# A linear-attention and top-1 MoE block on one core: low parts moved to VectorE, statistics to ScalarE, and a unit's last transposes moved behind two products

## The chip, the core and the metric

The kernel runs on one core of a Trainium2 chip. The core has five engines that run beside each other, each through its own list of instructions in order: TensorE (PE, matrix products; PEld is its loading of the stationary operand), VectorE (DVE), ScalarE (ACT), GpSimd (POOL) and SyncE (SP, which only issues transfers here). They wait for each other through semaphores. Data lies in HBM, in the on-chip memory SBUF (128 partitions), and in PSUM, where TensorE leaves its results in banks. The metric is the device time of one launch in microseconds; less is better.

## The reference

The input x has 2048 tokens of 512 numbers. The block is attention and then a mixture of experts, each added to its input:

```python
h  = x + A(layernorm(x))          # 32 heads of 16
h2 = h + B(layernorm(h))          # 8 experts, one per token

# A: q, k, v = x @ wqkv;  pq = q @ w_phi[head], pk = k @ w_phi[head]
#    phi = concat(softmax(p), softmax(-p))              over the 16 of a head
#    num = phi_q @ (phi_k^T v);  den = phi_q . sum(phi_k) + 1e-6
#    out = (num / den) @ wo
# B: expert = argmax(x @ w_gate);  out = silu(x @ w1[e]) @ w2[e]   (512 -> 1792 -> 512)
#    times a softmax over the one kept logit
```

## The kernel before

**Products in three parts.** Operands of the large products are split into a high part in the fp32r format (an ACT copy, `hi_of`) and the low rest (a subtraction, `lo_of`), and each product is three matmuls: high by high, high by low and low by high (`mm3`, the lines 75 to 77). So every activation and every weight needs one pass on ACT and one subtraction, mostly on DVE.

**Attention.** The 2048 tokens are sixteen chunks of 128. For each chunk the first loop (`s_ln`, `s_tr`, `s_k`, `s_v`, `s_q`, `feat1`, `feat2`, `s_kv`, `s_qt`) normalises x, transposes it, forms k, v, q, and the softmax features; `s_kv` adds phi_k^T v and the sums of phi_k into `kvps` in PSUM. The value product also carries eight more columns, the gate's weights applied to the normalised x (`xwg`), and `s_v` adds a correction with x's mean and the column sums `csg` of the gate on POOL.

**Second half and routing.** A second loop runs over c from 0 to 23 with stages in a pipeline: `s_num(c)` forms num and den and divides, `s_ot(c-1)` transposes and splits the result (PE `pto`, ACT `xh`, DVE `xl`), and `s_wo(c-2)` multiplies by wo (`po`; its PSUM tile has one buffer, so the next one waits until DVE has read it), adds x to give h (`hb`), forms gate logits `lg`, takes mean and variance of h by bn_stats and bn_aggr (`ln_rstd`), and corrects the logits by the mean. Each pair of chunks then has `s_top` (argmax, a one-hot `oh`, running counts `cum`, the gate on POOL, and a transfer of h to `hbuf` in HBM), `s_rank` (each token's rank in its expert: the small products `pl`; then one-hot rows `am` and `bm`) and `s_inv` (a product `acc` that builds the inverse list of tokens by expert). After half the tokens, `s_star` picks the commonest expert so far; the transfers of its weights `raw` start, and at c = 12 to 15 `split_chunk` splits four chunks of them (2048 columns each, in four pieces of 512), with ten of the sixteen low parts on POOL and six on DVE. `s_first` gathers that expert's first 128 tokens, and `prework(0)` normalises them on DVE (`xn`) and transposes them (`mtr`).

**Units.** A unit is 128 tokens of one expert; 19 run here. A unit has the first product in four blocks of columns (`gemm1`, tile `mh`), silu on ACT (`hs`), transposes of each block (`tr`: PE `mtr`, ACT `hThi`, DVE `hTlo`), and the second product (`g2`, tile `my`) of fourteen steps of three matmuls; DVE scales and adds h (`yo`), and POOL scatters the rows to the output. A unit also transposes the next unit's input (`prework(u + 1)`), and, where the next unit has a new expert, splits that expert's weights (`split`, in a branch that is taken by a flag). The PSUM tiles `mh` and `mtr` share four banks in turn (`bank`).

**What sets the order.** The program is written in the order of the loops; a scheduler then places the instructions on each engine's list within what their dependencies allow, so the lists do not follow the source line by line. Each list is fixed when the program is built.

Of the kernel before, what the change touches and what calls it, by code (L numbers as in the profile page):

```python
# [9 lines left out]
F32 = mybir.dt.float32  # L10
# [31 lines left out]
def kernel(  # L42
# [19 lines left out]
    def bc(ap, n):  # L62
        return ap.unsqueeze(len(ap.shape)).to_broadcast(list(ap.shape) + [n])
# [26 lines left out]
    G.iota(iotaS, pattern=[[P, NT]], base=0, channel_multiplier=0, allow_small_or_imprecise_dtypes=True)  # L90
    tok1 = consts.tile([P, NT], F32, name="tok1")
    G.iota(tok1, pattern=[[P, NT]], base=1, channel_multiplier=1, allow_small_or_imprecise_dtypes=True)
# [74 lines left out]

    LO = (V,) * NW

    def split_chunk(c, lo=None, n=2):  # L170
        for i in range(n):
            w = slice(i * (CW // n), (i + 1) * (CW // n))
            hi_of(whi[c][:, w], raw[c][:, w])
            eng = lo or LO[c]
            eng = eng[i] if isinstance(eng, tuple) else eng
            eng.tensor_tensor(wlo[c][:, w], raw[c][:, w], whi[c][:, w].bitcast(F32), op=OP.subtract)  # L176

# [14 lines left out]
    with ExitStack() as actx:  # L192
# [10 lines left out]
        wolo = keep.tile([P, KD, 2, HC], F32R, name="wolo")  # L203
        csg = keep.tile([P, 2, E // 2], F32, name="csg")
        xwg = keep.tile([P, NT, 2, E // 2], F32, name="xwg")
        kvbd = keep.tile([P, NG, 68], F32, name="kvbd")
        V.memset(kvbd, 0.0)
# [53 lines left out]
        def s_num(c):  # L261
            load_x(c)
            o = row("o", 2, "pc").rearrange("p (h f) -> p h f", f=DH)
            for i in range(2):
                pn = bank("pn")
                for g in range(4):
                    T.matmul(pn[:, g * 68:(g + 1) * 68], phT[c][:, 4 * i + g, :], kvbd[:, 4 * i + g, :],  # L267
                             start=True, stop=True)
                nv = pn[:, 0:272].rearrange("p (h f) -> p h f", f=DH + 1)
                den = work.tile([P, 16, 1], F32, name="den")  # L270
                V.tensor_scalar(den, nv[:, :, DH:DH + 1], 1e-6, None, op0=OP.add)
# [10 lines left out]
        if True:  # L282
# [116 lines left out]
            for k in range(KD):  # L399
                T.matmul(pc[:, 0:E], onesf, wgs[:, k, :], start=(k == 0), stop=(k == KD - 1))  # L400
            V.tensor_copy(csg.rearrange("p i e -> p (i e)"), pc[:, 0:E])

# [6 lines left out]
            for c in range(NT - 1):  # L409
# [7 lines left out]
                if c == 3:  # L417
                    pg = bank("pog")
                    for dt in range(KD):
                        for t in range(4):  # L420
                            T.matmul(pg[:, dt * E:(dt + 1) * E], woT_raw[t // 2][:, t % 2, dt * P:(dt + 1) * P],
                                     wgs[:, t, :], start=(t == 0), stop=(t == 3))
                    split_w(wo_raw, pg[:, 0:KD * E].rearrange("p (t i e) -> p t i e", t=KD, i=2), wohi, wolo)
# [33 lines left out]
        def s_wo(c):  # L457
# [11 lines left out]
            V.tensor_tensor(lg, po[:, :, D // 2:HC], xwg[:, c], op=OP.add)  # L469
            ln_rstd(h[:, 0:D], h[:, D:D + 2], h[:, D + 1:D + 2])  # L470
            V.scalar_tensor_tensor(lg, csg, h[:, D:D + 1], lg, op0=OP.mult, op1=OP.subtract)

        def s_top(b):
            hb, lg = bt[b]["hb"], bt[b]["lg"]
            mn = work.tile([P, NB, 1], F32, name="tmn")
            V.tensor_reduce(mn, lg, AX.X, OP.min)
            eq = work.tile([P, NB, E], F32, name="eq")
            V.tensor_tensor(eq, lg, mn.to_broadcast([P, NB, E]), op=OP.is_equal)
            V.tensor_tensor(eq, eq, mid(desc8, NB), op=OP.mult)
# [9 lines left out]
            nr = work.tile([P, NB, 1], F32, name="nr")  # L489
            V.tensor_reduce(gt[:, 0], mn, AX.X, OP.min)  # L490
            G.tensor_tensor(gt[:, 0], gt[:, 0], mn, op=OP.subtract)
            G.tensor_tensor(gt[:, 0], gt[:, 0], hb[:, :, D + 1:D + 2], op=OP.mult)
# [6 lines left out]
        def s_rank(b):  # L499
# [16 lines left out]
            bm = work.tile([P, NB, E, NT], F16, name="bm")  # L516
            for j in range(NB):
                c = b * NB + j
                V.tensor_scalar(am[:, j, :], iota128, sl[:, j:j + 1], None, op0=OP.is_equal)
                jm = work.tile([P, NT], F16, name="jm")  # L520
                V.tensor_scalar(jm, iotaS, bs[:, j:j + 1], tok1[:, c:c + 1], op0=OP.is_equal, op1=OP.mult)
                V.tensor_tensor(bm[:, j], bc(oh[:, j, :], NT), mid(jm, E), op=OP.mult)
            bt[b]["am"], bt[b]["bm"] = am, bm
# [33 lines left out]
        for c in range(NT + 8):  # L557
# [60 lines left out]
    def load_fl(a, b):  # L618
        _, v = nc.values_load_multi_w_load_instructions(isnew[0:1, a:b],
                                                        engines=[ENG.Activation, ENG.DVE, ENG.Pool])  # L620
        fls.update(zip(range(a, b), v))
# [97 lines left out]
    def unit(u):  # L719
# [43 lines left out]
        if u == 0:  # L763
            tr(3)
            split_chunk(4, V)
            with after(first_[0]):
                split_chunk(5, V)
                g2(py, 0, 8)
                xi = prework(1)
            with after(xi):  # L770
                split_chunk(6, V)
                index(3, 4, raw[1])
# [6 lines left out]
        else:  # L779
            if u + 1 < NU:  # L780
# [73 lines left out]
```

## Time and profile before

| | us |
|---|---|
| median of 3 runs | 735.6 (734.75 to 735.78) |
| the profiled execution | 732.92 |
| its span, first to last instruction | 731.2 |
| PE busy in the span | 702.0 |
| DVE busy | 468.8 |
| ACT busy | 303.2 |
| POOL busy | 180.8 |

"Busy" is the time in which an engine had an instruction in work. Matmuls are pipelined and overlap, so a busy PE can still be waiting in part; the granted clock tells how fast PE was allowed to run. In rows of groups, the numbers behind the bar are the time all instructions of a group were busy, the mean of one in ns, and the idle time of the engine just before them with what ended it. In rows of the timeline they are the start and the duration in us.

### The profile page before, as it was taken

How to read it: one execution, taken by the hardware profiler on the slowest of the kernel's cores; microseconds unless marked ns; L12 is line 12 of the kernel's file. 1: busy time of each engine (PE TensorE's matmuls, PEld its weight loads, DVE VectorE, ACT ScalarE, POOL GpSimd, SP SyncE). 2: the span in 40 equal slices, each digit the busy share in tenths (PEclk: the TensorE clock that was granted, in tenths of full speed). 3: DMA queues.
4: the chain of work that ended last, by engine and by line, in shares of the span. 5: the costliest groups of instructions: out<-in, count | busy, mean ns of one | idle time of the engine just before them, and what ended most of it. 6: DMA issues, size and time to landing. Idle time of an engine off the chain costs nothing.

```text
span 731.2 us, 12523 instructions
## 1 busy us (share of the span) xinstructions
PE 702.0 (96%) x4130; PEld 612.2 (84%) x4130; DVE 468.8 (64%) x969; ACT 303.2 (41%) x458; POOL 180.8 (25%) x281
## 2 busy tenths in 40 slices
PE   6999999999999998779999999999999999999996
PEld 6899999999989997658888888888888878888885
DVE  4996987878787889794512999972185472922211
ACT  4534444434322015152112888862274463822211
POOL 3364645434313328521110011110011111011110
PEclk9999999999999999899999999999999999999999
DMA  9111101100002249417400799981066381001000
GB/s 332 57 30 44 30 15 30 30 15 1 1 16 73 74 156 341 153 34 294 193 29 2 258 369 376 344 345 53 30 210 241 121 328 31 11 29 30 30 30 6
DMA packets 21912, 87.61 MB, mean 120 GB/s; under 512 B 3070, under 2 KB 3582, under 8 KB 14656
## 3 DMA queue, kind: packets, MB, share of 16 engines
q1 hardware_dynamic: 18624, 76.86, 28.8%
q0 software_dynamic: 3200, 9.75, 4.0%
q8 instruction: 34, 0.56, 0.3%
q14 instruction: 54, 0.44, 0.2%
HBM read 78.18 MB, written 9.21 MB: 120 GB/s over the span
## 4 chain that ended last, share of the span: by engine, by line
issue 46%; PE 35%; DMA 10%; DVE 6%; POOL 1%; ACT 1%; POOLq 1%; SPq 0%; DVEq 0%
DMA out_dram<-yo,sidx 8%; PE kvps L372 4%; PE pn L267 3%; PE pq L75 2%; PE pq L77 2%; PE pq L76 2%; PE ptq L381 2%; PE pv L77 2%; PE pv L76 2%; PE pv L75 2%; PE pk L75 2%; PE pk L77 2%; PE pk L76 2%; PE po L75 2%; PE po L76 2%
## 5 line engine op out<-in xcount | busy, mean ns | idle before, releaser
L69 ACT ACTIVATE whi<-raw 128x1024 fp32r<-128x1024 f32 (+1 forms) x120 | 118.7, 1003 | 67.9 <-PE mh L77 37.4
L176 DVE TENSOR_TENSOR wlo<-raw,whi 128x1024 fp32r<-128x1024 f32 (+1 forms) x110 | 130.6, 1200 | 18.6 <-ACT whi L69 12.5
L75 PE MATMUL mh<-whi,xhi 128*128 128x512 f32 (+1 forms) x304 | 114.9, 378 | 0.0
L77 PE MATMUL mh<-whi,xlo 128*128 128x512 f32 (+1 forms) x304 | 111.5, 367 | 0.0
L76 PE MATMUL mh<-wlo,xhi 128*128 128x512 f32 (+1 forms) x304 | 111.4, 366 | 0.0
L798 POOL DMA_INDIRECT out_dram<-yo,sidx x19 | 21.5, 1131 | 352.5 <-DVEq L635 202.0
L76 PE MATMUL my<-wlo,hThi 128*128 128x512 f32 x266 | 104.7, 393 | 3.5 <-DVE wlo L176 3.3
L75 PE MATMUL my<-whi,hThi 128*128 128x512 f32 x266 | 106.0, 399 | 0.3 <-ACT hThi L69 0.3
L77 PE MATMUL my<-whi,hTlo 128*128 128x512 f32 x266 | 104.6, 393 | 0.3 <-DVE hTlo L72 0.3
L72 DVE TENSOR_TENSOR hTlo<-mtr,hThi 128x512 fp32r<-128x512 f32 x76 | 47.0, 621 | 86.2 <-ACTq L635 53.3
L163 ACT ACTIVATE hs<-mh 128x512 f32<-128x512 f32 x76 | 41.0, 540 | 145.3 <-PE mh L77 145.3
L355 POOL TENSOR_TENSOR ph<-t,sm 128x1024 f32<-128x1024 f32 x32 | 62.1, 1939 | 66.9 <-DVE sm L353 37.8
L77 PEld LDWEIGHTS mh<-whi,xlo 128*128 128x128 f32 x304 | 57.2, 188 | 10.2
L76 PEld LDWEIGHTS mh<-wlo,xhi 128*128 128x128 f32 x304 | 57.3, 189 | 9.3
L75 PEld LDWEIGHTS mh<-whi,xhi 128*128 128x128 f32 x304 | 57.2, 188 | 9.3
L797 DVE SCALAR_TENSOR_TENSOR yo<-my,xg 128x512 f32<-128x512 f32 x19 | 14.2, 748 | 78.4 <-PE my L77 78.4
L76 PEld LDWEIGHTS my<-wlo,hThi 128*128 128x128 f32 x266 | 50.3, 189 | 14.2 <-DVE wlo L176 4.3
L77 PEld LDWEIGHTS my<-whi,hTlo 128*128 128x128 f32 x266 | 50.3, 189 | 11.2 <-DVE hTlo L72 0.5
L75 PEld LDWEIGHTS my<-whi,hThi 128*128 128x128 f32 x266 | 50.4, 189 | 10.5 <-ACT hThi L69 0.5
L352 DVE TENSOR_REDUCE sm<-t 128x64 f32<-128x1024 f32 x32 | 38.8, 1214 | 12.0 <-ACT t L347 11.9
L727 PE MATMUL mtr<-ident,hs 128*128 128x128 f32 x266 | 41.7, 274 | 2.7 <-DVE hTlo L72 2.6
L347 ACT ACTIVATE t<-t 128x1024 f32<-128x1024 f32 x32 | 33.9, 1061 | 20.9 <-DVE t L346 19.8
(206 smaller groups left out, 1407.3 us busy)
## 6 DMA issues: line engine op xcount, KB each, us to landing
raw<-in_w_dram SPq DMA_DIRECT2D x56, 1024.0 KB, 5.2
xt<-in_x_dram SPq DMA_DIRECT2D x32, 256.0 KB, 2.7
hbuf<-hb SPq DMA_DIRECT2D x8, 516.0 KB, 3.8
phT<-in_wqkT_dram SPq DMA_DIRECT2D x4, 512.0 KB, 5.1
phT<-in_wv_dram SPq DMA_DIRECT2D x2, 512.0 KB, 6.4
phT<-in_wo_dram SPq DMA_DIRECT2D x2, 512.0 KB, 8.2
phT<-in_woT_dram SPq DMA_DIRECT2D x2, 512.0 KB, 5.6
xg<-hbuf,gidx POOLq DMA_INDIRECT x21, 3.7
```

Of the source, the lines that this page charges most:

```text
L69: A.activation(dst, src, AF.Copy)
L72: V.tensor_tensor(dst, src, hi.bitcast(F32), op=OP.subtract)
L75: T.matmul(ps, ahi, bhi, start=first, stop=False)
L76: T.matmul(ps, ahi, blo, start=False, stop=False)
L77: T.matmul(ps, alo, bhi, start=False, stop=last)
L163: A.activation(hs[c % 2][:, 0:fw], p[:, 0:fw], AF.Silu)
L176: eng.tensor_tensor(wlo[c][:, w], raw[c][:, w], whi[c][:, w].bitcast(F32), op=OP.subtract)
L347: A.activation(t, t, AF.Exp)
L352: V.tensor_reduce(sm, t, AX.X, OP.add)
L355: G.tensor_tensor(ph.rearrange("p (a f) -> p a f", f=DH), t, bc(sm, DH), op=OP.mult)
L372: T.matmul(kvps[g // 4][:, g % 4, :], ph[:, g * P:(g + 1) * P], vt[:, 4 * g:4 * g + 4, :].rearrange("p h f -> p (h f)"), start=(c == 0 and ...
L727: T.transpose(pt[:, j * P:(j + 1) * P], hs[c % 2][:, j * P:(j + 1) * P], ident)
```

## The change

It has seven edits. (1) `split_chunk` uses `lo_of` for all low parts, so POOL does none; POOL is taken out of the flags that the branches read. (2) In `s_wo`, h's mean and variance come from two ACT passes with a summed output (a copy, and a square of h minus the mean), with small POOL steps between and after them that form the negative mean, the mean, the variance plus epsilon and its power. (3) The gate's weights have their column mean subtracted before they go through wo (`wgc`), so that the corrections by the mean of x and of h, and the negation, are gone; the argmax looks for the largest logit. (4) The epsilon of the denominator is added to `kvbd` once instead of to each `den`. (5) The one-hot rows of two chunks are made by four instructions on both at once. (6) `tok1` is float16. (7) In a unit, `tr(3)` stands after `g2(py, 0, 2)`.

```diff
-    LO = (V,) * NW
-    def split_chunk(c, lo=None, n=2):
+    def split_chunk(c, n=2):
         for i in range(n):
             w = slice(i * (CW // n), (i + 1) * (CW // n))
             hi_of(whi[c][:, w], raw[c][:, w])
-            eng = lo or LO[c]
-            eng = eng[i] if isinstance(eng, tuple) else eng
-            eng.tensor_tensor(wlo[c][:, w], raw[c][:, w], whi[c][:, w].bitcast(F32), op=OP.subtract)
+            lo_of(wlo[c][:, w], raw[c][:, w], whi[c][:, w])
...
-                split_chunk(c - NT + 4, ((G, G, V, V), (G, G, G, V), (G, G, G, V), (G, G, V, V))[c - NT + 4], 4)
+                split_chunk(c - NT + 4, 4)
...
-                V.tensor_scalar(den, nv[:, :, DH:DH + 1], 1e-6, None, op0=OP.add)
-                V.reciprocal(den, den)
+                V.reciprocal(den, nv[:, :, DH:DH + 1])
...
-                mc = work.tile([P, 2, E // 2], F32, name="mc")
-                G.tensor_scalar(mc, csg, st[c]["mv"][:, 0:1], None, op0=OP.mult)
-                G.tensor_tensor(xwg[:, c], xwg[:, c], mc, op=OP.add)
...
+            wgc = wp.tile([P, KD, E], F32, name="wgc")
+            csg = wp.tile([P, E], F32, name="csg")
+            V.tensor_scalar(csg, pc[:, 0:E], 1.0 / D, None, op0=OP.mult)
+            V.tensor_tensor(wgc, wgs, mid(csg, KD), op=OP.subtract)
...
-                    V.tensor_copy(kvbd[32 * h:32 * h + 32, 4 * i:4 * i + 4, 17 * h:17 * h + 17],
-                                  kvps[i][32 * h:32 * h + 32, :, 17 * h:17 * h + 17])
+                    V.tensor_tensor(kvbd[32 * h:32 * h + 32, 4 * i:4 * i + 4, 17 * h:17 * h + 17],
+                                    kvps[i][32 * h:32 * h + 32, :, 17 * h:17 * h + 17],
+                                    epsz[32 * h:32 * h + 32], op=OP.add)
...
-            ln_rstd(h[:, 0:D], h[:, D:D + 2], h[:, D + 1:D + 2])
-            V.scalar_tensor_tensor(lg, csg, h[:, D:D + 1], lg, op0=OP.mult, op1=OP.subtract)
+            junk = row("junk", 3, "xn")
+            sm = work.tile([P, 2], F32, name="hsum")
+            A.activation(junk, h[:, 0:D], AF.Copy, accum_out=sm[:, 0:1])
+            nm = work.tile([P, 1], F32, name="hnm")
+            G.tensor_scalar(nm, sm[:, 0:1], -1.0 / D, None, op0=OP.mult)
+            G.tensor_scalar(h[:, D:D + 1], sm[:, 0:1], 1.0 / D, None, op0=OP.mult)
+            A.activation(junk, h[:, 0:D], AF.Square, bias=nm, accum_out=sm[:, 1:2])
+            ve = work.tile([P, 1], F32, name="ve")
+            G.tensor_scalar(ve, sm[:, 1:2], 1.0 / D, EPS, op0=OP.mult, op1=OP.add)
+            G.tensor_tensor(h[:, D + 1:D + 2], ve, nhalf, op=OP.pow)
...
-            for j in range(NB):
-                c = b * NB + j
-                V.tensor_scalar(am[:, j, :], iota128, sl[:, j:j + 1], None, op0=OP.is_equal)
-                jm = work.tile([P, NT], F16, name="jm")
-                V.tensor_scalar(jm, iotaS, bs[:, j:j + 1], tok1[:, c:c + 1], op0=OP.is_equal, op1=OP.mult)
-                V.tensor_tensor(bm[:, j], bc(oh[:, j, :], NT), mid(jm, E), op=OP.mult)
+            jm = work.tile([P, NB, NT], F16, name="jm")
+            V.tensor_tensor(jm, mid(iotaS, NB), bc(bs, NT), op=OP.is_equal)
+            V.tensor_tensor(jm, jm, bc(tok1[:, b * NB:(b + 1) * NB], NT), op=OP.mult)
+            V.tensor_tensor(bm, bc(oh, NT), jm.unsqueeze(2).to_broadcast([P, NB, E, NT]), op=OP.mult)
+            V.tensor_tensor(am, mid(iota128, NB), bc(sl, P), op=OP.is_equal)
...
                 prework(u + 1)
+            g2(py, 0, 2)
             tr(3)
-            g2(py, 0, 2)
```

More of the change, by code (lines that the diff above doesn't have):

```diff
@@ L90 @@
     G.iota(iotaS, pattern=[[P, NT]], base=0, channel_multiplier=0, allow_small_or_imprecise_dtypes=True)
-    tok1 = consts.tile([P, NT], F32, name="tok1")
+    tok1 = consts.tile([P, NT], F16, name="tok1")
     G.iota(tok1, pattern=[[P, NT]], base=1, channel_multiplier=1, allow_small_or_imprecise_dtypes=True)
@@ L203 @@
         wolo = keep.tile([P, KD, 2, HC], F32R, name="wolo")
-        csg = keep.tile([P, 2, E // 2], F32, name="csg")
         xwg = keep.tile([P, NT, 2, E // 2], F32, name="xwg")
+        epsz = keep.tile([P, 4, DH + 1], F32, name="epsz")
+        V.memset(epsz, 0.0)
+        V.memset(epsz[:, :, DH:DH + 1], 0.5e-6)
         kvbd = keep.tile([P, NG, 68], F32, name="kvbd")
@@ L421 @@
                             T.matmul(pg[:, dt * E:(dt + 1) * E], woT_raw[t // 2][:, t % 2, dt * P:(dt + 1) * P],
-                                     wgs[:, t, :], start=(t == 0), stop=(t == 3))
+                                     wgc[:, t, :], start=(t == 0), stop=(t == 3))
                     split_w(wo_raw, pg[:, 0:KD * E].rearrange("p (t i e) -> p t i e", t=KD, i=2), wohi, wolo)
@@ L469, in s_wo @@
             V.tensor_tensor(lg, po[:, :, D // 2:HC], xwg[:, c], op=OP.add)
-            ln_rstd(h[:, 0:D], h[:, D:D + 2], h[:, D + 1:D + 2])
-            V.scalar_tensor_tensor(lg, csg, h[:, D:D + 1], lg, op0=OP.mult, op1=OP.subtract)
+            junk = row("junk", 3, "xn")
[8 more added lines that the diff above has]
+            G.tensor_tensor(h[:, D + 1:D + 2], ve, nhalf, op=OP.pow)
         def s_top(b):
             hb, lg = bt[b]["hb"], bt[b]["lg"]
-            mn = work.tile([P, NB, 1], F32, name="tmn")
-            V.tensor_reduce(mn, lg, AX.X, OP.min)
+            mx = work.tile([P, NB, 1], F32, name="tmx")
+            V.tensor_reduce(mx, lg, AX.X, OP.max)
             eq = work.tile([P, NB, E], F32, name="eq")
-            V.tensor_tensor(eq, lg, mn.to_broadcast([P, NB, E]), op=OP.is_equal)
+            V.tensor_tensor(eq, lg, mx.to_broadcast([P, NB, E]), op=OP.is_equal)
             V.tensor_tensor(eq, eq, mid(desc8, NB), op=OP.mult)
@@ L489, in s_top @@
             nr = work.tile([P, NB, 1], F32, name="nr")
-            V.tensor_reduce(gt[:, 0], mn, AX.X, OP.min)
-            G.tensor_tensor(gt[:, 0], gt[:, 0], mn, op=OP.subtract)
+            V.tensor_reduce(gt[:, 0], mx, AX.X, OP.max)
+            G.tensor_tensor(gt[:, 0], mx, gt[:, 0], op=OP.subtract)
             G.tensor_tensor(gt[:, 0], gt[:, 0], hb[:, :, D + 1:D + 2], op=OP.mult)
@@ L619, in load_fl @@
         _, v = nc.values_load_multi_w_load_instructions(isnew[0:1, a:b],
-                                                        engines=[ENG.Activation, ENG.DVE, ENG.Pool])
+                                                        engines=[ENG.Activation, ENG.DVE])
         fls.update(zip(range(a, b), v))
@@ L764, in unit @@
             tr(3)
-            split_chunk(4, V)
+            split_chunk(4)
             with after(first_[0]):
-                split_chunk(5, V)
+                split_chunk(5)
                 g2(py, 0, 8)
@@ L770, in unit @@
             with after(xi):
-                split_chunk(6, V)
+                split_chunk(6)
                 index(3, 4, raw[1])
```

1 line of the change is left out of this document (removed).

## The prediction

> **What bounds the kernel now.** I read the page's busy shares, then the sums by stretch of time, the waits of TensorE (PE), and last the timeline where PE is not full.
>
> ```profile
> PE 702.0 (96%) x4130; PEld 612.2 (84%) x4130; DVE 468.8 (64%) x969; ACT 303.2 (41%) x458; POOL 180.8 (25%) x281
> ```
> ```profile
> 26.00:205.00 179.00, 179.00 (x1186) 163.34 (x1184) 144.51 (x232) 74.42 (x118) 82.32 (x115) 0.99 0.07 22
> ...
> 225.00:266.00 41.00, 40.98 (x366) 40.46 (x364) 33.50 (x156) 5.81 (x10) 15.26 (x42) 1.00 0.29 90
> ...
> 280.00:302.20 22.20, 16.56 (x101) 15.35 (x102) 21.43 (x70) 6.26 (x12) 20.30 (x32) 0.77 0.69 245
> 302.20:317.70 15.50, 15.50 (x102) 12.92 (x100) 10.91 (x51) 4.30 (x6) 4.78 (x12) 1.00 0.29 115
> ...
> 336.20:731.20 395.00, 385.51 (x1944) 322.35 (x1942) 198.55 (x265) 180.84 (x260) 39.09 (x37) 1.00 0.41 152
> ```
>
> The columns after the length are PE, weight loads, VectorE (DVE), ScalarE (ACT) and GpSimd (POOL), then granted clock, DMA share and GB/s. PE is full in attention (26 to 205 us), in the output projections (225 to 266) and from 302 to 318. Between 280 and 302, where the first expert's weights are split while the last tokens are routed, DVE is full (21.43 of 22.20), POOL nearly so, PE has 16.56 and a granted clock of 0.77. An edit pays there, or where PE itself waits:
>
> ```profile
> PE mtr L727 <- DVE hTlo L72: 2.6, 7, 0.4
> PE pl L504 <- DVE oh L483: 2.5, 1, 2.5
> PE po L75 <- DVE lg L469: 2.3, 2, 1.9
> ```
>
> The last two lie inside 280 to 302. The first is seven times 0.4 us in the expert units.
>
> **The change, part by part. 1: all low parts on DVE.** Ten of sixteen subtractions leave POOL. First, what they cost DVE today:
>
> ```profile
> 283.67 1.31 DVE L519 TENSOR_SCALAR am<-iota,sl 128x128 f16<-128x128 f32 x1
> ```
> ```profile
> 283.56 3.80 POOL L176 TENSOR_TENSOR wlo<-raw,whi 128x512 fp32r<-128x512 f32 x3
> ```
> ```profile
> L519 DVE TENSOR_SCALAR am<-iota,sl x16: 273/279/1307, 236.9 to 315.8; 128x128 f16<-128x128 f32 x16
> ```
> ```profile
> L471 DVE SCALAR_TENSOR_TENSOR lg<-csg,hb,lg x16: 216/226/1243, 218.1 to 311.2; 128x8 f32<-128x8 f32 x16
> ```
> ```profile
> L479 DVE TENSOR_TENSOR eq<-eq,desc x8: 110/170/1089, 226.7 to 312.9; 128x16 f32<-128x16 f32 x8
> ```
> ```profile
> L222 DVE BATCH_NORM_STATS2 bs<-hb 128x6 f32<-128x512 f32 x3 | 2.1, 695 | 0.0
> ...
> L471 DVE SCALAR_TENSOR_TENSOR lg<-csg,hb,lg 128x8 f32<-128x8 f32 x3 | 1.7, 564 | 0.0
> L519 DVE TENSOR_SCALAR am<-iota,sl 128x128 f16<-128x128 f32 x2 | 1.6, 794 | 0.0
> L521 DVE TENSOR_SCALAR jm<-iotaS,rb,tok 128x16 f16<-128x16 f32 x2 | 1.6, 779 | 0.0
> L522 DVE TENSOR_TENSOR bm<-oh,jm 128x128 f16<-128x128 bf16 x2 | 1.4, 688 | 0.0
> ...
> L479 DVE TENSOR_TENSOR eq<-eq,desc 128x16 f32<-128x16 f32 x1 | 1.1, 1089 | 0.0
> L483 DVE TENSOR_TENSOR oh<-eq,km 128x16 bf16<-128x16 f32 x1 | 0.9, 942 | 0.0
> L271 DVE TENSOR_SCALAR den<-pn 128x16 f32<-128x16 f32 x4 | 0.7, 162 | 0.0
> ```
>
> The last fence groups DVE from 277.5 to 299. An `am` that normally takes 0.28 us takes 1.31 beside a POOL subtraction. With 0.28 as the quiet time of am, jm and bm the surplus is 2 x (0.794 + 0.779 + 0.688) - 6 x 0.28 = 2.84; for lg 3 x (0.564 - 0.226) = 1.01; for eq and oh 1.089 + 0.942 - 2 x 0.17 = 1.69. Together 5.5 us of DVE time that POOL causes.
>
> The Trainium skill (SBUF — State Buffer, section "Who interferes with whom") says that a DVE instruction with two SBUF inputs, or in a two-port mode, and a GpSimd instruction that reads SBUF exclude each other for a whole instruction. On the wide subtractions the trace agrees (1.31 against 0.28).
>
> Now the sum for this stretch, along DVE's order:
>
> ```profile
> 280.13 0.68 DVE L466 TENSOR_TENSOR hb<-po,xt 128x512 f32<-128x512 f32 x1
> ...
> 296.97 0.16 DVE L469 TENSOR_TENSOR lg<-po,xwg 128x8 f32<-128x8 f32 x1
> ...
> 298.38 0.66 DVE L176 TENSOR_TENSOR wlo<-raw,whi 128x512 fp32r<-128x512 f32 x1
> ...
> 299.18 0.54 DVE L144 TENSOR_SCALAR xn<-xg 128x512 f32<-128x512 f32 x1
> ```
> ```profile
> 297.27 0.56 PE L75 MATMUL po<-wohi,xh 128*128 128x260 f32 x1 [1.94 <-DVE lg L469]
> 302.16 0.61 PE L147 MATMUL mtr<-ident,xn 128*128 128x128 f32 x4
> ```
>
> From hb (280.13) to the last lg before the transposes (297.13) are 17.0 us. Off: 5.5 of surplus, and two rounds of statistics and mean correction with the four `den` additions, 2 x 0.695 + 2 x 0.226 + 0.7 = 2.5, of which about 2.2 is start to start. On: in the built order eight low parts stand ahead of that lg instead of two, 6 x 0.66 = 4.0. So lg comes at 17.0 - 5.5 - 2.2 + 4.0 = 13.3 us, 3.7 earlier. xn: 19.05 before; 5.5 and 3.2 (three rounds) off, 8 x 0.66 = 5.3 on, 15.65, so 3.4 earlier, at about 296. The path then runs lg, projection `po`, `mtr`: 302.16 - 297.27 = 4.9 us at the reduced clock. With that clock kept, mtr starts at 298.4, a gain of 3.7. At the full rate `po` takes 24 x 0.12 = 2.9 (two neighbouring products below start 0.12 apart), mtr starts when xn is done at 296.3, and the gain is 5.9.
>
> ```profile
> 291.82 0.28 PE L77 MATMUL po<-wohi,xl 128*128 128x260 f32 x1
> 291.94 0.28 PE L75 MATMUL po<-wohi,xh 128*128 128x260 f32 x1
> ```
>
> I take 4.8, the middle of the two: PE idles less in this stretch but does not stop idling. DVE stays its bound, so nothing hides an instruction there. The ends are 5.9 and, if ACT cannot deliver the high parts in time, 0.
>
> **2: statistics of h on ACT.** Sixteen bn_stats and bn_aggr leave DVE (counted above where DVE is the bound, worth 0 where PE is full). ACT gets 32 passes over 128x512 with a sum; POOL's two small steps per chunk become four.
>
> ```profile
> L69 ACT ACTIVATE xh<-pto 128x512 fp32r<-128x512 f32 x8 | 4.8, 598 | 35.1 <-PE pto L237 25.9 <-DVE den L271 4.6 <-DVE eq L479 4.6
> ```
> ```profile
> L232 ACT ACTIVATE xn<-xt,nbias,rstd 128x512 f32<-128x512 f32 x16 | 13.1, 819 | 17.5 <-POOL nbias L231 17.5
> ...
> L225 POOL TENSOR_SCALAR ve<-hb 128x1 f32<-128x1 f32 x16 | 4.4, 272 | 31.5 <-DVE tmn L476 14.2 <-DVE den L271 6.7 <-DVE rk L509 3.7
> ```
>
> Price of a pass: low 0.60 (the copy xh), high 0.82 (xn, which also scales and shifts) plus a read of the sum, say 0.9; I take 0.75, nearer the plain copy. ACT then has, per chunk in the projection stage, 0.73 (5.81 over 8 xh) plus 1.5 of 5.1 us (41.0 / 8): it is covered by PE's full queue, cost 0. New is a wait inside ACT's order: the second pass waits for POOL's mean, and behind it stand the next chunk's xh, phT and, from 280 on, whi. Who waits for those is PE's `po`, through xl, and DVE's wlo. The mean takes 0.27 on POOL plus queueing; POOL is busy 1.9 us a chunk (15.26 / 8), so the whole is at worst 0.73 + 1.8 + 0.27 + 1.9 = 4.7 us, under 5.1. Between 280 and 302 ACT has 6.26 of 22.2 busy; 8 more passes make 12 or 13. Cost 0, high end in the rivals. The last q features (ph of chunk 15) now stand on POOL behind the statistics of chunk 0, about 1 us later, while PE reaches them a projection later too: 0.
>
> **3: paired one-hots, centred gate weights, epsilon in kvbd.** Six one-hot instructions per pair of chunks become four wider ones; the two sides are within 0.3 us per pair, two pairs in the stretch: 0, ends -0.6 and +0.6. Two small DVE steps at the start replace 32 POOL steps, whose wait on ACT held up only POOL while PE was full (179.00 of 179.00): 0. Eight adds replace eight copies before kvbd: 0. SP's list moves one load of x by one place: 0.
>
> **4: a unit's last transposes behind two products.**
>
> ```profile
> 446.32:468.23 21.91, 21.53 (x110) 17.90 (x109) 20.63 (x23) 18.74 (x24) 2.72 (x2) 1.00 0.92 358
> 509.24:530.59 21.35, 21.35 (x109) 17.94 (x108) 4.30 (x7) 4.51 (x9) 2.00 (x2) 1.00 0.08 25
> ```
> ```profile
> 433.24 0.68 DVE L72 TENSOR_TENSOR hTlo<-mtr,hThi 128x512 fp32r<-128x512 f32 x1
> ...
> 530.59 0.75 DVE L797 SCALAR_TENSOR_TENSOR yo<-my,xg 128x512 f32<-128x512 f32 x1 [7.47 <-PE my L77]
> ```
> ```profile
> 434.07 0.41 PE L727 MATMUL mtr<-ident,hs 128*128 128x128 f32 x2 [0.37 <-DVE hTlo L72]
> ```
>
> The windows run from one yo to the next: a unit that splits the next expert's weights takes 21.91, one that does not 21.35. The 0.56 is the seven-fold wait: the transposes need a PSUM bank that hTlo of the second block frees at 433.92. Six products of 0.23 put ahead of them take 1.4 us and need only the first block of hT; the bank is then free 1.0 us early. Seven units x 0.56 = 3.9. In units without splits the same instructions run, 0. On ACT the last hThi now stands behind the first whi pair (2.1 us) and DVE's hTlo behind that; they are needed by product 12 of 14, 7 us later: hidden. DVE is 20.63 busy of 21.91, so in the run of four such units it may lag 0.2 us more per unit than PE; the 1.0 covers it. Bounds 0 and 3.9; taken 3.8.
>
> **Sum.** 4.8 + 3.8 = 8.6. The profiled execution took 732.9 (span 731.2): 724.3. The runs' median is 735.6, 2.7 above it; from there **727.0 us**.
>
> **The rivals.** (a) The wait in the units is replaced: DVE lags and PE stops at the next bank. For it: DVE's 20.63 of 21.91; against it: three of the seven split units stand alone and can catch up afterwards. 735.6 - 4.8 = 730.8. (b) ACT becomes the bound of the split stretch: whi stands behind statistics that wait for hb and POOL, so DVE gains nothing there. For it: ACT is in order and leads every wlo; against: 13 of 22 us. 735.6 - 3.8 = 731.8. (c) Slower: in the projection stage xh of the next chunk is held back behind the second pass until PE waits for `po`. It decides from 8.6 / 14 = 0.6 us per chunk over 5.1, so when ACT's turn reaches 5.7; at 6.0 it is 14 x 0.9 = 12.6, giving 739.6. For it: POOL's 1.9 us per chunk come in blocks; against: the 4.7 above. (d) Neither works: 735.6. (e) PE's clock is not lowered again: gain 5.9 there, 725.9. (f) POOL's two added steps per chunk hold DVE up as the wide ones did: four chunks in the stretch x 2 x 0.27 = 2.2, giving 729.2. Against it, beside a small POOL step DVE is not stretched:
>
> ```profile
> 300.77 0.82 POOL L493 TENSOR_TENSOR gt<-euler,gt 128x2 f32<-128x2 f32 x1
> ```
> ```profile
> 300.75 0.28 DVE L522 TENSOR_TENSOR bm<-oh,jm 128x128 f16<-128x128 bf16 x1
> ```
>
> [...]
>
> **How the numbers follow.** Forecast with (e): 0.55; (a) 0.09; (b) 0.12; (f) 0.05; (d) 0.05; (c) 0.14. Alone, the forecast spans 725 to 729. The range 723.5 to 732.5 takes in (a), (b) and (f), 0.81, with 1.5 us below (e) for one-hots that come out cheaper and a lowered clock elsewhere. About 0.2% (1.5 us) is what a measurement of this kernel can tell from no change. Faster 0.81, same 0.05, slower 0.14.
>
> **What would show it.** Between the split's first hb and mtr: no wlo on POOL, am near its 0.28 median in every row or once per pair at 128x256 without stretching, mtr near 297. In the units: no row of mtr waiting for hTlo, split units near 21.4. Wrong, if PE's waits list xh or xl in the projection stage (c), if DVE's waits list whi from 280 on (b), or if a new wait on DVE as long as 0.4 appears in split units (a).

## The result, and the profile after

The changed kernel takes 723.0 us (722.57 to 723.8) against 735.2 beside it (734.17 to 735.78): a ratio of 0.9837 (0.982 to 0.9854), a gain of 12.2 us. Forecast were 8.6 of gain and 727.0 us, range 723.5 to 732.5: the direction and the places are right, the size is too small, and the time lies just below the range. The profiled execution takes 722.8 us (span 721.0).

The busy line of the page, and then the sums by stretch (length, PE, weight loads, DVE, ACT, POOL, clock, DMA share, GB/s):

```profile
PE 697.6 (97%) x4130; PEld 606.6 (84%) x4130; DVE 450.6 (63%) x886; ACT 324.2 (45%) x522; POOL 171.7 (24%) x271
```
```profile
226.50:267.50 41.00, 41.00 (x369) 40.63 (x368) 27.39 (x122) 16.27 (x41) 19.16 (x59) 1.00 0.31 99
278.70:295.13 16.43, 13.58 (x105) 13.05 (x104) 15.12 (x51) 10.44 (x24) 8.64 (x19) 0.91 0.73 273
295.13:311.20 16.07, 15.82 (x103) 13.14 (x103) 10.24 (x53) 7.49 (x15) 7.26 (x20) 0.98 0.32 110
329.62:714.43 384.81, 384.77 (x1944) 321.11 (x1942) 197.18 (x265) 180.07 (x260) 38.14 (x36) 1.00 0.42 157
```

The four rows are the projection stage, the split stretch (from the hb behind which the weights are split to the first mtr), the stretch after it, and the units. The projection stage is as full as before. From the split's hb to the first unit's transposes 22.0 us have become 16.4, DVE still at 92% there. From the first yo to the last, 388.2 have become 384.8, with PE full. PE's waits, the chain that the forecast followed (DVE's and PE's rows), and one split unit from yo to yo:

```profile
PE my L76 <- DVE wlo L72: 3.3, 1, 3.3
PE po L75 <- DVE lg L467: 2.6, 2, 2.1
```
```profile
278.70 0.68 DVE L464 TENSOR_TENSOR hb<-po,xt 128x512 f32<-128x512 f32 x1
...
290.56 0.16 DVE L467 TENSOR_TENSOR lg<-po,xwg 128x8 f32<-128x8 f32 x1
290.63 2.49 DVE L72 TENSOR_TENSOR wlo<-raw,whi 128x512 fp32r<-128x512 f32 x4
...
293.12 0.54 DVE L144 TENSOR_SCALAR xn<-xg 128x512 f32<-128x512 f32 x1
```
```profile
290.86 0.36 PE L75 MATMUL po<-wohi,xh 128*128 128x260 f32 x1 [2.06 <-DVE lg L467]
...
295.13 0.74 PE L147 MATMUL mtr<-ident,xn 128*128 128x128 f32 x3
```
```profile
L527 DVE TENSOR_TENSOR am<-iota,sl x8: 412/418/425, 238.6 to 307.1; 128x256 f16<-128x256 f32 x8
```
```profile
418.09:439.47 21.38, 21.38 (x110) 17.88 (x109) 20.47 (x23) 18.46 (x24) 2.72 (x2) 1.00 0.94 364
```

The wait of mtr for hTlo is gone, the split unit takes 21.38 in place of 21.91, am is never stretched. By stage, with the first row of pn at 205.29 before and 206.83 after: start 1.5 us longer; pn to mtr 96.9 to 88.3; mtr to first yo 34.0 to 34.5; units 388.2 to 384.8. That makes 10.0 of the 10.1 us between the two profiled executions; before's profiled execution lay 2.3 below its median here, which is the rest.

### The profile page after: what moved, and what is told of

Its sections match the earlier page's. It is cut to its first block, busy times and chain, and to the rows that moved or that the text cites. A ratio compares the mean times of both kernels' runs of the same rounds, so it can differ in the third digit from the quotient of the medians.

```text
span 721.0 us, 12308 instructions
## 1 busy us (share of the span) xinstructions
PE 697.6 (97%) x4130; PEld 606.6 (84%) x4130; DVE 450.6 (63%) x886; ACT 324.2 (45%) x522; POOL 171.7 (24%) x271
## 5 line engine op out<-in xcount | busy, mean ns | idle before, releaser
L72 DVE TENSOR_TENSOR wlo<-raw,whi 128x1024 fp32r<-128x1024 f32 (+1 forms) x120 | 135.9, 1151 | 15.8 <-ACT whi L69 8.1
L69 ACT ACTIVATE whi<-raw 128x1024 fp32r<-128x1024 f32 (+1 forms) x120 | 118.1, 1001 | 60.4 <-PE mh L77 43.6
L75 PE MATMUL mh<-whi,xhi 128*128 128x512 f32 (+1 forms) x304 | 114.6, 377 | 0.2 <-ACT xhi L69 0.2
L75 PE MATMUL my<-whi,hThi 128*128 128x512 f32 x266 | 107.7, 405 | 0.2 <-ACT hThi L69 0.2
L69 ACT ACTIVATE hThi<-mtr 128x512 fp32r<-128x512 f32 x76 | 41.1, 542 | 11.7 <-PE mtr L732 11.6
```

The lines of the kernel that those rows point to most:

```text
L69: A.activation(dst, src, AF.Copy)
L72: V.tensor_tensor(dst, src, hi.bitcast(F32), op=OP.subtract)
L75: T.matmul(ps, ahi, bhi, start=first, stop=False)
```

## The experiments

Two numbers are read from each run: its ratio to the kernel before on the same chip, and in its profile the stretch from the first pn (a numerator product of the second half) to the first yo (the first unit's output), 130.9 us before and 122.8 after. Some theories are put for pn to mtr (the first transposes of a unit's input), 96.9 and 88.3. One execution of that stretch is uncertain by some 1.5 us, as the second profile of the changed kernel shows below.

**One edit alone or taken back.** Theories first: the lock by POOL's wide subtractions (T1), or the earlier request for the first expert's weights (T2), which the changed profile shows (267.2 in place of 270.2).

Units only:
```diff
+            g2(py, 0, 2)
             tr(3)
-            g2(py, 0, 2)
```


> The kernel before with one edit: in each unit from the second on, the transposes of the last block stand behind the first two products of the second stage. Theory A (the forecast's term for the units is right, and the rest of the gain is made ahead of them): seven split units x 0.56 us = 3.9, so about 731.3 against 735.2, split units near 21.4 and no transpose waiting for hTlo. Theory B (the 3.4 us that the two profiles show between first and last yo is only part of it, the reordering being worth the 3.6 us by which the forecast fell short as well): 7 us or more, under 728.5. Rival (a) of the forecast: a wait on DVE takes its place, about 735.


Measured: 0.9947 (0.9926 to 0.9969), 3.9 us; pn to first yo 131.1, units 384.7. Theory A: the units' term is right and ends there.

Low parts only:
```diff
...
-                split_chunk(c - NT + 4, ((G, G, V, V), (G, G, G, V), (G, G, G, V), (G, G, V, V))[c - NT + 4], 4)
+                split_chunk(c - NT + 4, 4)
```


> The kernel before with one edit: all low parts of the first expert on DVE, none on POOL. Theory T1 (POOL's wide subtractions are what costs; the whole 8.6 us by which the changed profile is shorter between 205 us and the transposes of the first unit comes from taking them away): 6 to 9 us faster, about 727 to 729, and the wait of the projection's transposes for DVE's xl near 278 us (2.1 us) gone. Theory T2 (that wait went because the first expert's weights are asked for 3 us earlier, which the statistics' move does): the request stays at 270.2, the wait stays, and of the stretch only the forecast's share remains, 5.5 of surplus against six added subtractions of 0.66 on DVE's path to lg, some 1.5 us: about 733.7, at the ends 731 and 735.2.


Measured: 1.0003 (0.9981 to 1.0024); pn to first yo 131.2. T1 falls: without the lock the kernel is no faster.

The same edit taken back from the changed kernel:

> The changed kernel with ten of sixteen low parts back on POOL. T1: it loses most of the 8.6 us, 729 to 731. T2: the weights are still asked for at 267, so the wait near 278 stays away; lost is the forecast's share of the low parts, about 1.5 us and at most 3.7: 724.5, up to 726.7.


Measured: 0.9927 (0.9905 to 0.9949), 728.4 us, 5 to 6 slower than the changed kernel; pn to first yo 126.8. T2 falls: the weights are asked for as early as in the changed kernel (60.5 us behind the first pn, 60.4 there), and yet more than its 3.7 us is lost. The low parts are worth nothing alone, and 4 to 6 us here.

Statistics taken back:
```diff
...
-            A.activation(junk, h[:, 0:D], AF.Copy, accum_out=sm[:, 0:1])
...
+            ln_rstd(h[:, 0:D], h[:, D:D + 2], h[:, D + 1:D + 2])
```


> The changed kernel with the statistics of h back on DVE (bn_stats and bn_aggr), all else as changed. T1: it loses the forecast's share of the statistics, 2.2 us on DVE's path to lg: about 725.2, and no wait of the transposes for xl near 278. T2: the product that counts the tokens moves back behind the projection, the weights are asked for at about 270 again, the wait of about 2 us near 278 and the lowered clock behind it (1.7 us) return: 2.2 + 3.8 = 6.0, about 729.


Measured: 0.9896 (0.9846 to 0.9947); 123.8, and the wait before pto only 0.4 us. T2 falls again.

So another theory, D: from some 62 us behind the first pn, a little ahead of the landing of the first expert's weights, to the end of xn DVE is the bound, and what counts is everything on its list, wherever it stands. The sums by stretch for that part, before and after:

```profile
267.29:299.72 32.43, 24.82 (x183) 23.14 (x182) 30.65 (x113) 11.16 (x20) 23.52 (x35) 0.88 0.73 265
```
```profile
268.83:293.66 24.83, 21.98 (x186) 21.35 (x185) 23.09 (x83) 16.62 (x37) 15.12 (x30) 0.97 0.82 325
```

DVE idles 1.8 us in both; all 7.6 us between them are work. Some 2.3 of these did not go away: one hb, two reciprocals and the small steps that pick the expert stand ahead of the window in the changed kernel. And in the window's first part PE is full as well: up to 276.0 before (8.71 of 8.71 us), and up to the hb at 278.70 after (9.87 of 9.87, DVE 8.13). That DVE is the bound there too is argued, not shown. DVE's groups before, then after:

```profile
L176 DVE TENSOR_TENSOR wlo<-raw,whi 128x512 fp32r<-128x512 f32 x6 | 4.6, 782 | 1.8 <-ACT whi L69 1.8
L222 DVE BATCH_NORM_STATS2 bs<-hb 128x6 f32<-128x512 f32 x5 | 3.5, 693 | 0.0
...
L471 DVE SCALAR_TENSOR_TENSOR lg<-csg,hb,lg 128x8 f32<-128x8 f32 x5 | 2.1, 428 | 0.0
...
L271 DVE TENSOR_SCALAR den<-pn 128x16 f32<-128x16 f32 x8 | 1.3, 164 | 0.0
...
L223 DVE BATCH_NORM_AGGREGATE hb<-bs 128x2 f32<-128x6 f32 x5 | 0.9, 174 | 0.0
```
```profile
L72 DVE TENSOR_TENSOR wlo<-raw,whi 128x512 fp32r<-128x512 f32 x16 | 10.3, 683 | 1.4 <-ACT whi L69 1.4
...
L527 DVE TENSOR_TENSOR am<-iota,sl 128x256 f16<-128x256 f32 x2 | 0.8, 414 | 0.0
L526 DVE TENSOR_TENSOR bm<-oh,jm 128x256 f16<-128x256 bf16 x2 | 0.8, 414 | 0.0
```

Five rounds of statistics, five corrections of lg and eight additions stand in it, where the forecast had counted three, three and four. With the low parts alone, what the lock gives back, ten more subtractions take: 30.58 busy of 32.37.

```profile
267.66:300.03 32.37, 25.76 (x189) 24.44 (x188) 30.58 (x122) 11.04 (x20) 15.73 (x25) 0.88 0.80 294
```

**The edits priced at little or nothing.**
```diff
...
+            V.tensor_tensor(wgc, wgs, mid(csg, KD), op=OP.subtract)
...
-            V.scalar_tensor_tensor(lg, csg, h[:, D:D + 1], lg, op0=OP.mult, op1=OP.subtract)
```


> The kernel before with one edit: the gate weights are centred at the start, so lg is no longer corrected by the mean of h, and the top-1 does not wait for the statistics. The stretch from the first numerator product (pn) to the first transposes of the units (mtr) was 96.9 us before, 88.3 after, 96.1 with the low parts alone. Theory P (the forecast: this edit is worth nothing): 96.9 less the few 0.23 us steps that leave DVE's list, 96.2 to 96.9, time within 0.7 us of before. Theory G (the edit priced at 0 carries the missing gain, because it takes the statistics out of the chain from hb to the top-1, and so out of the way of the first expert's number and its weights): 93 to 94, 3 to 4 us faster.


Measured: 1.0001 (0.998 to 1.0022), theory P's time; but pn to mtr 93.6, theory G's stretch. From pn to the first yo it is 128.7: 2.2 us gained there and given back in the start, 2.0 us longer in this profile, 1.1 of them in attention (see Addresses).

> The changed kernel with the gate weights as they were: lg is corrected by the mean of h, which now comes from ScalarE and GpSimd. Theory P: the stretch from pn to mtr stays at 88.3 to 89, time as after. Theory G: the top-1 waits for two passes of ScalarE and GpSimd's step, and behind it DVE's whole list; 92 or more, at least 3.5 us slower than after.


Measured: 0.9925 (0.9898 to 0.9952), 727.2 us, 4 to 6 slower than after; pn to mtr 90.3, to first yo 124.8. Theory G in sign and near its size.

> The changed kernel with the one-hots made for one chunk at a time again (six instructions a pair in place of four). Forecast: the two sides within 0.3 us a pair, two pairs in the stretch, so pn to mtr 88.3 plus or minus 0.6. If the paired form carries part of what was missed: 90 or more.


Measured: 0.9876 (0.9816 to 0.9935), median 721.6; pn to mtr 86.4, to first yo 121.6: the paired form gains nothing that these profiles resolve, as forecast.

> The changed kernel with the epsilon added to each denominator again (32 additions on DVE, 0.16 us each, four or five of them in the full stretch). Forecast: 4 x 0.16 = 0.7, pn to mtr 89.0. If the shorter way from pn to the transposes of the same chunk (pto stands some 1.3 us earlier in the changed kernel from the eleventh chunk on) carries part of what was missed: 90 to 91.


Measured: 0.9855 (0.982 to 0.989); pn to mtr 89.6, to first yo 124.1, 1.3 to 2.9 longer than after. The time does not resolve it.

The epsilon alone:
```diff
-                V.tensor_scalar(den, nv[:, :, DH:DH + 1], 1e-6, None, op0=OP.add)
-                V.reciprocal(den, den)
+                V.reciprocal(den, nv[:, :, DH:DH + 1])
...
```


> The kernel before with one edit: epsilon inside kvbd, no addition to the denominators. Forecast (priced within the statistics' 2.5 at 0.7 for four additions): pn to first yo 130.2 in place of 130.9. Theory D (DVE's list is the bound from the landing of the first expert's weights on, so eight additions count there, 8 x 0.16 to 0.24, and the transposes of each chunk come earlier): 128.0 to 129.3. Taking it out of the changed kernel cost 2.9 there.


Measured: 1.0026 (1.0008 to 1.0043), 0.3% slower, with a start 1.8 us longer in its profile; pn to first yo 130.1, near the forecast's 0.7 and within the scatter. So theory D's number for a single edit is wrong. DVE idles no more than before (1.2 us in the window of theory D); what grows there are its own six low parts, stretched beside POOL's ten (4.6 us before, 782 ns each):

```profile
L176 DVE TENSOR_TENSOR wlo<-raw,whi 128x512 fp32r<-128x512 f32 x6 | 7.5, 1262 | 1.1 <-ACT whi L69 1.1
```

**Do they need each other?** Three edits together (low parts, statistics, gate):

> The kernel before with three edits together: low parts on DVE, statistics on ScalarE, gate weights centred; the one-hots, the epsilon and the units' order as before. The low parts alone and the gate alone measured 0, each taken out of the changed kernel cost 4 to 6.5 us. Theory S (they only pay together, since each leaves DVE as the bound of the same stretch): 6 to 8 us faster than before, about 727, pn to mtr about 89. Theory L (the effects add up; the single ones are what they measured alone, and the rest was the statistics' 4.3): 730 or more, pn to mtr 92 or more.


Measured: 0.9939 (0.9915 to 0.9962), 729.0; pn to mtr 89.9, to first yo 124.8. By stage theory S, by time between the two: 4.8 us.

> The kernel before with two edits: the statistics on ScalarE and the gate weights centred; the low parts stay with GpSimd as before. Theory Q (ScalarE's second pass waits for GpSimd's mean, which stands behind wide subtractions, and with ScalarE wait xh and the high parts: the statistics on ScalarE pay only with the low parts gone from GpSimd): pn to first yo no better than with the gate alone, 128.5 to 130 us, and about 10 us of ScalarE's waits for GpSimd between the landing of the weights and mtr. Rival (the edits add up): 128.7 less the 2.6 that taking the statistics out of the changed kernel cost, 126.1.


Measured: 0.9992 (0.9972 to 1.0011), 128.1: close to theory Q, 0.6 us from the gate alone. ACT's waits, from 268 us on, in this run, in the run with the low parts taken back, and in the changed kernel; then POOL in the run with the low parts taken back:

```profile
ACT junk L475 <- POOL hnm L473: 10.1, 3, 4.8
```
```profile
ACT junk L478 <- POOL hnm L476: 10.5, 4, 5.0
```
```profile
ACT junk L474 <- POOL hnm L472: 5.7, 4, 1.8
```
```profile
281.34 4.20 POOL L176 TENSOR_TENSOR wlo<-raw,whi 128x512 fp32r<-128x512 f32 x3
285.51 0.23 POOL L476 TENSOR_SCALAR hnm<-hsum 128x1 f32<-128x1 f32 x1
```

With wide subtractions on POOL, the mean of h (0.23 us) waits 4.2 us in POOL's order, and ACT's second pass behind it. So far theory Q is right. But that this wait is what costs is not shown: DVE's own waits do not lead back to it. In the run with the low parts taken back DVE idles 4.2 us of its stretch (28.07 us, 23.83 busy), for these reasons:

```profile
270.31:298.38 28.07, 23.11 (x172) 22.32 (x172) 23.83 (x74) 15.66 (x35) 23.94 (x36) 0.82 0.75 294
```
```profile
DVE raw L685 <- POOL wlo L176: 2.5, 1, 2.5
DVE hb L468 <- PE po L77: 1.5, 2, 1.2
```

The longer of them is a small step that waits for POOL's subtraction itself. In the run with the statistics and the gate (first row) DVE waits for ACT's high parts hardly longer than in the changed kernel (second row):

```profile
DVE wlo L176 <- ACT whi L69: 1.7, 2, 1.5
```
```profile
DVE wlo L72 <- ACT whi L69: 1.4, 1, 1.4
```

What the traces do show is a lock that is not a fixed price. With the low parts taken back DVE has ten subtractions fewer than in the changed kernel, and yet 0.7 us more to do: its other steps take 17.9 us in place of 12.8, and its own six low parts are stretched too:

```profile
L176 DVE TENSOR_TENSOR wlo<-raw,whi 128x512 fp32r<-128x512 f32 x6 | 5.9, 1012 | 0.1
```

Nor is it shown that the low parts pay only with the statistics on ACT. With the statistics back on DVE (above) the stretch is still 7.1 us shorter than before, more than the other edits brought one by one: the gate 2.2, the epsilon 0.8, the low parts nothing, the one-hots nothing that was resolved. So the edits do help each other, but which needs which stays open: the low parts with the gate alone, for one, were not run.

**Dose and clock.** The changed kernel again, then with four to eight low parts moved behind xn:

> The changed kernel itself, to see how much of the stages differs from execution to execution. Theory R (the forecast's remainder is in the run, not in the kernel): the start up to pn, 206.8 us in the first profile and 205.3 to 208.3 in those of the other kernels, and the number of stretches of 3.4 us at half clock change by 1 to 2 us from profile to profile, and the median of more runs lies at 723 to 726. Theory K (the kernel does it): pn to mtr stays at 88.3 within 0.7 us and the median at 722.5 to 723.5.


Measured: 722.2 (721.67 to 723.05); 0.9854 (0.9822 to 0.9886); pn to mtr 87.0. The median is the kernel's, as theory K has it, though 0.3 below its range; pn to mtr lies 1.3 off, more than theory K allows. There the half clock during the last `po` (below) did not come in this execution (granted clock 1.00 from 289.1 to 294.3).

```diff
-            if NT - 4 <= c < NT:
+            if NT - 4 <= c < NT - 2:
                 split_chunk(c - NT + 4, 4)
...
             if c == NT - 1:
                 prework(0)
+            if c == NT - 1:
+                split_chunk(2, 4)
+            if c == NT:
+                split_chunk(3, 4)
```


> The changed kernel with the split of the third and fourth chunk of weights put behind the first unit's normalised tokens (xn): four of DVE's low parts leave the way to the lg that the projection before mtr waits for, four more the way to xn. Theory D (from the landing of the weights to mtr DVE is the bound, and each microsecond of its list counts once): 4 x 0.62 = 2.5 us, pn to mtr 85.8 in place of 88.3, and as much in the time, if the products of the first unit do not then wait for the low parts (DVE is idle for about 5 us between 294 and 310). Rival (the low parts are late next, or the bound is PE's clock and not DVE): pn to first yo unchanged at 122.8, time as after.


Measured: 720.6 (720.21 to 720.85), 0.9828 (0.9796 to 0.986); pn to first yo 118.7 against 121.3 of the second profile of after: 2.5 us, theory D's price, and 1.6 in the time. (pn to mtr is 81.8, but a projection has moved behind mtr.) The low parts that moved stand behind the split's hb, so this shows DVE as the bound from there on. The stretch, DVE idle 1.75:

```profile
270.97:290.30 19.33, 18.54 (x162) 18.15 (x162) 17.58 (x70) 15.42 (x34) 10.21 (x22) 1.00 1.00 389
```

Products of no use in two of PE's waits (two more steps of the second product stand ahead of the second filling):
```diff
...
+                with tc.issue_after(lp.ins):
+                    for k in range(16):
+                        T.matmul(fl[:, 0:HC], wohi[:, 0, 0, 0:P], wohi[:, 1, 0, :], start=True, stop=True)
...
+                for k in range(14):
+                    T.matmul(fl, hThi[2][:, 0, :], w2_at(whi, 8), start=True, stop=True)
```


> The changed kernel with products of no use put into two of PE's waits: 16 of 128x260 (16 x 0.12 = 1.9 us) in the wait of 2.1 us for lg before the last projection ahead of mtr, and 14 of 128x512 (14 x 0.23 = 3.3) in the wait of 3.3 us for wlo in the first unit. Theory C (a PE that stands still gets half its clock some microseconds later, for 3.4 us, at a cost of 1.7): the half clock at 292.2 to 295.6 and at 322.9 to 326.4 is gone, pn to mtr 87, mtr to first yo 32.8, time 2.5 to 3.4 us less than after. Rival (the half clock comes by itself, whatever PE did): stages and time as after, or longer by what the products overrun the waits.


Measured: 722.3 (721.48 to 723.46), 0.9857 (0.9825 to 0.9889); pn to mtr 87.0, pn to first yo 121.3, all as in the second profile of after. In the first unit, after again and then with the filling:

```profile
316.83:325.32 8.49, 5.16 (x17) 3.81 (x16) 7.25 (x27) 0.69 (x1) 3.26 (x2) 0.80 0.21 62
```
```profile
316.00:325.45 9.45, 8.03 (x35) 5.59 (x33) 8.12 (x29) 1.79 (x3) 3.26 (x2) 1.00 0.20 56
```
```profile
316.81 3.36 PE L781 MATMUL fl<-whi,hThi 128*128 128x512 f32 x14
...
324.24 0.63 PE L147 MATMUL mtr<-ident,xn 128*128 128x128 f32 x4 [0.71 <-DVE nxt L709]
325.45 0.50 PE L76 MATMUL my<-wlo,hThi 128*128 128x512 f32 x1 [0.59 <-DVEq L645]
```

The granted clock goes from 0.80 to 1.00, so here a PE kept busy kept it. But it buys nothing; PE then waits for DVE, 0.71 and 0.59 us, which the slow clock had covered. The first part of theory C holds in this place, its price falls.

**Addresses.** Attention is longer in the changed kernel, though nothing in it waits longer. One row each for the 44 transposes of xn, first and last start: before, after, after with a table padded, before with a table padded:

```profile
L237 PE MATMUL pt<-ident,xn x44: 270/272/273, 72.9 to 187.5; 128*128 128x128 f32 x44
```
```profile
L235 PE MATMUL pt<-ident,xn x44: 270/272/273, 73.2 to 188.9; 128*128 128x128 f32 x44
```
```profile
L235 PE MATMUL pt<-ident,xn x44: 270/273/273, 72.8 to 188.2; 128*128 128x128 f32 x44
```
```profile
L237 PE MATMUL pt<-ident,xn x44: 270/273/277, 73.7 to 189.3; 128*128 128x128 f32 x44
```
```diff
-    tok1 = consts.tile([P, NT], F16, name="tok1")
+    tok1 = consts.tile([P, 2 * NT], F16, name="tok1")[:, 0:NT]
```


> The changed kernel with one small table (tok1) padded by 32 bytes a row; the instructions and their order are the same on every engine, only SBUF addresses move: the weights of the projections then start at a multiple of 64 bytes, as before the change, in place of 32 beyond one. Theory A (the address makes the attention stage longer): chunks of 11.43 us in place of 11.53, some 1.3 us less up to pn, 720.9 in the median. Rival (the longer chunks come from the change's instructions): chunks 11.53, time as after, 722.2.


Measured: 722.3 (720.32 to 723.26), 0.9847 (0.9826 to 0.9867). The 44 rows span 115.4 us; they had spanned 114.6 before and 115.7 after. Theory A as put falls: a start at a multiple of 64 does not bring the short chunks back.

> The kernel before with tok1 padded by 32 bytes a row, so that its projection weights start 32 bytes beyond a multiple of 64; nothing else changed. Theory A (address): chunks of 11.53 in place of 11.43 and 1.3 us more, ratio 1.002. Rival: chunks 11.43 and ratio 1.000.


Measured: 1.0007 (0.9992 to 1.0021). The rows span 115.6 in place of 114.6, from a shift alone; and the units take 386.8 in place of 388.2. So addresses do move both stages by about 0.4 to 1%, here in opposite directions. Which tile's address it is stays open.

The single edits carry the same microsecond. With the gate alone the 44 rows span 115.7 us and with the epsilon alone 115.5, though the epsilon's edit changes no instruction of that loop; with the low parts alone they span 114.6, and with the epsilon or the one-hots taken back from the changed kernel 114.8 and 114.9. So what an edit is worth is better read from the stretch than from the time.

**A faster version.** The padding and the later chunks together:

> The changed kernel with the same padding and with the split of the third and fourth chunk of weights behind the first unit's xn. If the two findings add up, 720.6 - 1.3 = 719.3; if the padding does nothing, 720.6.


Measured: 719.8 (718.44 to 723.0), 0.9823 (0.9801 to 0.9845); 118.7. No more than the later chunks alone.

```diff
-            G.tensor_scalar(nm, sm[:, 0:1], -1.0 / D, None, op0=OP.mult)
+            A.activation(nm, sm[:, 0:1], AF.Copy, scale=-1.0 / D)
```


> The changed kernel with the third and fourth chunk's split behind xn, and with the negative mean made by ScalarE itself in place of GpSimd (a copy of 128x1 with a scale). Theory Q: the 4 us of waits for hnm leave ScalarE; DVE waits for the high parts for 1.4 us there, so up to 1.4 us less than with the later chunks alone (720.6): 719.2 to 720.6. Rival (the small pass on ScalarE costs as much as the wait): 720.6 or more.


Measured: 719.1 (717.54 to 719.9), 0.9802 (0.9776 to 0.9828), with the later chunks and without the padding: the lowest median, 14 us below before. No wait of ACT for hnm is left; pn to first yo 119.1, not shorter than with the chunks alone, so what the mean brings is not resolved.

## Why the prediction was wrong in size

- **Units, 3.8: right.** 3.4 by stage, 3.9 by the run with that edit alone. No wait took its place; rival (a) is out.
- **The split stretch, 4.8: this step failed,** first by where it starts. The sum ran from hb at 280.13, and what comes ahead of that was put at nothing. But hb itself comes 3.0 us earlier, counted from pn (280.13 - 205.29 = 74.8; 278.70 - 206.83 = 71.9). Before, PE waited there for xl, at 279.93, in a row of the waits that the forecast left out:

```profile
PE pto L237 <- DVE xl L72: 2.0, 1, 2.0
```

  In the changed kernel that wait is gone. Which edit took it away stays open: with the low parts alone it is gone too, and nothing is gained.
- **The same stretch, from hb on: mis-sized.** From hb to the last lg the forecast had 13.3 us; it is 12.0 (290.56 + 0.16 - 278.70), 5.0 saved in place of 3.7. The sum left out the two bn_aggr (0.35) and the stretching of DVE's own low parts (one took 1.17 us at 290.12, 0.5 too long), and the paired one-hots take 1.2 us there in place of the 1.7 left for them. From po to mtr 4.9 became 4.3 in the first profile and 3.0 in the second: the two ends that were averaged are two executions of one kernel. Together with hb that is 8.6 and 9.9 in place of 4.8.
- **The gate and the epsilon: too small.** The heading of part 3 puts them at 0, but DVE's share of them stands in part 1: two corrections of lg at 0.45, four `den` additions at 0.7. The gate alone brought 2.2 us in the stretch, taken back it cost 2.0 to 3.6; the epsilon brought 0.8 alone, which is within the scatter, and cost 1.3 to 2.9 taken back. Why the epsilon costs more taken back than it brought alone is not shown. The paired one-hots bring nothing that the run without them resolves.
- **1 and 2 were summed as if each edit had one price.** Low parts: 5.5 of surplus against 4.0 of added work gave 1.5. Alone the edit is worth 0, as all ten subtractions count (6.6) and not six more; taken back from the changed kernel it costs 4 to 6. The lock's 5.5 was read from one list of DVE; with another list beside the same ten subtractions it is another number (1.01 and 1.26 us for a low part of DVE, 0.78 before). ACT's second pass waits for POOL 1.8 us at most in the changed kernel, as allowed for (1.9).
- **2: cost on ACT 0: right.** A pass takes 0.63 or 0.72 and reading its sum 0.19 (1.73 for two passes, forecast 1.5), and PE stays full in the projections. Rivals (b) and (c) are out.

```profile
L474 ACT ACTIVATE junk<-hb,hnm 128x512 f32<-128x512 f32 x16 | 11.5, 720 | 9.0 <-POOL hnm L472 8.9
L470 ACT ACTIVATE junk<-hb 128x512 f32<-128x512 f32 x16 | 10.0, 628 | 25.1 <-DVE hb L464 25.1
L474 ACT ACTIVATION_READ_ACCUMULATOR junk<-hb,hnm 128x1 f32 x16 | 3.0, 189 | 0.0
```

- **"Worth 0 where PE is full"**: the edits' instructions, yes; but attention became about 1 us longer. Addresses alone can do that, as the shifted kernel shows; whether they do it here stays open.
- **Rival (f)** is not borne out on DVE: am and bm take 0.41 in the stretch. It is POOL that is stretched now, beside a wlo of DVE that also starts at 273.02:

```profile
273.02 1.26 POOL L501 TENSOR_TENSOR nr<-gt,mone 128x2 f32<-128x2 f32 x1
...
298.28 0.73 POOL L501 TENSOR_TENSOR nr<-gt,mone 128x2 f32<-128x2 f32 x1
```

The Trainium skill (SBUF — State Buffer, "Who interferes with whom") says that the order of issue decides which of the two engines is held up. Two pairs shown ahead of the result agree: POOL's subtraction began at 283.56 and held the am of 283.67; bm began at 300.75, ahead of POOL's gt at 300.77, and kept its 0.28 us, while gt took 0.82 where its median is 0.70. So that second pair, which the forecast set against (f), shows only that DVE was first. In the row at 273.02 the starts are equal, so it does not tell which was first.

## What to carry to other kernels

Begin the sum at the first wait that the change can move, not where the stretch looks worst, and count everything on the bound engine's list from there; small steps off the obvious path are part of it. Do not take the price of one edit from one list and add it to the next: the low parts alone, and the statistics with the gate, measured 0 each (1.0003 and 0.9992), and the three together 4.8 us. In the one wait that was tried to the end, an engine's lower clock cost nothing, as the next wait was for another engine.

## What was not expected of the hardware

- A shift of SBUF addresses by 32 bytes, with no other change, made attention 1.0 us longer and the units 1.4 us shorter. In the other profiles with before's order of the units, these take 388.2 to 388.5 us.
- In two executions of the same kernel the half clock came during the last projection once (4.3 us) and once not (3.0). The Trainium skill (TensorE: Matmul & The Clock Gate, "Part 1: The HAM clock gate") says that the clock is decided in windows that run freely, so that one kernel differs from run to run; these two profiles agree. Filled with products, the wait in the first unit was followed by full clock (1.00 against 0.80).
